# A fused attention and MLP kernel on one core: the second MLP product as seven half-size products, and attention tiles normalised in pairs

## The chip, the core and the metric

The kernel runs on one core of a Trainium2 chip. The core has five engines that work at the same time and meet through semaphores: TensorE (PE, matrix products and transposes, results in PSUM), VectorE (DVE), ScalarE (ACT), GpSimd (POOL) and SyncE (SP, here only a queue that starts DMAs). The metric is the device time of one execution in microseconds. A matmul has a stationary operand, loaded first (row PEld of the profile), and a moving operand that streams past it. PSUM has eight banks of 512 fp32 values per partition.

## The reference

```python
scores = scale * (q @ k.T)                        # batch 8, heads 8, seq 576, head_dim 64
mask_local   = (rel >= 0) & (rel < 32)            # heads 0..3; rel = row - column
mask_strided = (rel >= 0) & (col % 32 == row % 32)  # heads 4..7
attn = softmax(where(mask, scores, -1e9))
x = (attn @ v) -> (4608 tokens, 512)
h = x @ w_in                                      # 512 -> 2048
g = h * tanh(log(1 + exp(h)))                     # "Mish"
out = g @ w_out                                   # 2048 -> 512, float32
```

## The kernel before, in words

The 4608 tokens are worked through in nine blocks of 512 (`for t in range(NBLK)`). Attention is worked through in eight batches of 576 tokens. Batch 0 is a prologue. From then on block t holds the attention of batch t+1 in the gaps of its MLP, so that blocks 0 to 6 carry attention and blocks 7 and 8 carry none. The order on every engine is the order in which the program emits instructions; nothing is reordered by a scheduler.

**A block has two stages.** In the first (`mlp1`, L426) PE makes h in eight groups of two 128-wide slices of the 2048. A group fills one "acc" (two PSUM banks), and ACT turns it into `gT` with one Mish activation (L431). There are three accs, x, y and z, used in turn. In the second stage (`mlp2`, L446) PE makes the output in four tiles of 128 tokens, each of 16 matmuls with 512 moving columns, emitted as 16 steps of four matmuls. After step i the attention pieces of `at[i]` are emitted. Block 8 uses `mlp2_last` (L473).

**Attention pieces.** `Q` (L276) makes scores in an acc, and ACT exponentiates them into P tiles (L281). A part is six or five such units: s0, s1 and s2 of the strided heads, l0, l1 and l2 of the local heads. `M` multiplies a part by the mask (L287, on DVE). `V` (`pv`, L303) multiplies one of 8 strided tiles or 6 local windows by v, four matmuls into one bank of a ring of two (`tile_t`). DVE then takes the reciprocal of the row sums (L314) and scales (L315) into `x_s` or `x_l`. `pv2` does the same for two tiles at once in an acc (L328, L329); before the change only the prologue uses it. `X` (`xt`, L342 and L352) transposes six or eight such tiles on PE into a bank of the ring, and ACT copies them to `xT` (L149), the input of the next `mlp1`.

**Queues.** SP's queue holds in this order for block t: the store of the first two token tiles (L454, after step 7), six DMA transposes of k and q of batch t+2 (L172 and L178, after step 9), the second store, then the loads of k, q and v of batch t+3 (L109, L115, L129). The transposes of the local heads read the bf16 copies that POOL casts (`cast_qk_loc`, `cast_v`, L151) from loaded float32. POOL's queue in block t holds these casts, emitted between the two stages, and then two DMA issues for batch t+3 (`load_qk_str`, L97).

PSUM in the second stage: acc z and one other hold the output, acc x and y take scores.

Of the kernel before, what the change touches and what calls it, by code (L numbers as in the profile page):

```python
# [10 lines left out]
F32 = mybir.dt.float32  # L11
# [27 lines left out]
def kernel(ctx, tc, q, k, v, moe_w_in, moe_w_out, out):  # L39
# [37 lines left out]
    x_l = const.tile([128, NW, 256], BF16, name="x_l")  # L77
    x_s = const.tile([128, CS, 256], BF16, name="x_s")

    g_pool = ctx.enter_context(tc.tile_pool(name="gp", bufs=2))  # L80
    small = ctx.enter_context(tc.tile_pool(name="small", bufs=4))
    o_pool = ctx.enter_context(tc.tile_pool(name="op", bufs=2))
    PS = bass.MemoryType.PSUM
# [277 lines left out]
    def attn_steps(b, x, y):  # L361

        a = Attn(b)
        Q = lambda i_acc, *parts: (lambda: a.qk(parts, i_acc))
        M = lambda kd, i: (lambda: a.mask(kd, i, nc.vector))
        V = lambda kd, i: (lambda: a.pv(kd, i))
        X = lambda kd, hf: (lambda: a.xt(kd, hf))
        s0, s1, sl2, l0, l1 = ("s", 0), ("s", 1), (("s", 2), ("l", 2)), ("l", 0), ("l", 1)
        if x == y:
            return [  # L370
                [], [Q(x, s0)],
                [M(*s0), Q(x, s1)],
                [V("s", 0)],
                [V("s", 1), M(*s1), Q(x, *sl2)],
                [V("s", 2)],
                [V("s", 3), M("s", 2), M("l", 2), Q(x, l0)],
                [V("s", 4)],
                [V("s", 5), M(*l0), Q(x, l1)],
                [V("s", 6), V("l", 5)],
                [V("s", 7), V("l", 0), M(*l1)],  # L380
                [X("s", 0), V("l", 1)],
                [X("s", 1), V("l", 2)],
                [V("l", 3), V("l", 4)],
                [X("l", 0), X("l", 1)], [],
            ]
        return [
            [],
            [Q(x, s0), Q(y, s1), M(*s0), M(*s1)],
            [],
            [V("s", 0), V("s", 1)],  # L390
            [Q(x, *sl2), Q(y, l0), V("s", 2)],
            [V("s", 3), M("s", 2), M("l", 2)],
            [V("s", 4), M(*l0)],
            [Q(x, l1), V("s", 5)],
            [V("s", 6), V("l", 5)],
            [V("s", 7), M(*l1)],
            [V("l", 0), V("l", 1)],
            [X("s", 0), V("l", 2)],
            [X("s", 1), V("l", 3)],
            [V("l", 4), X("l", 0)],  # L400
            [X("l", 1)], [],
        ]


# [7 lines left out]

    def mlp1(t, accs):
        gT = g_pool.tile([128, 16, 512], BF16, tag="gT", name="gT")

        held = {}

        def group(g, ccs=(2, 3, 0, 1)):
            if g not in held:
                held[g] = acc(accs[g % 3], "psh")  # L420
            ps = held[g]
            for u in range(2):
                fc = 2 * g + u
                for a, n, o in segs(t):
                    for cc in ccs:
                        nc.tensor.matmul(  # L426
                            ps[:, u, o:o + n], lhsT=w_in[:, cc, fc * 128:(fc + 1) * 128],
                            rhs=xT[:, cc, a:a + n], start=(cc == 2), stop=(cc == 1),
                        )
            if ccs[-1] == 1:  # L430
                nc.scalar.activation(gT[:, 2 * g:2 * g + 2, :], ps[:], AF.Mish)  # L431
        if t == 0:
            return gT, [lambda g=g, c=c: group(g, c) for c in ((2, 3), (0, 1)) for g in range(2)] + [
                lambda g=g: group(g) for g in range(2, 8)
            ]
        return gT, [lambda g=g: group(g) for g in range(8)]

    def mlp2(t, gT, accs, fc_major=False):
        po = {}
# [43 lines left out]
    with tc.manual_schedule():  # L483
# [12 lines left out]
        load_v_str(0)  # L496
        load_v_loc(0)
        load_qk_loc(1)
        lq0 = g_pool.tile([128, 16, 512], BF16, tag="gT", name="lq0")
        lq0 = lq0[:].rearrange("p a b -> p (a b)")[0:PL]  # L500
        kl0, ql0 = [lq0[:, 1536 * i:1536 * i + 1536].rearrange("p (h x) -> p h x", h=4) for i in range(2)]
        for p in P_l:
# [55 lines left out]
        nc.sync.dma_start(gate[:], w_in[0:1, 0, 1536:1792])  # L558
        load_v(1)
        accs = (2, 1, 0)  # L560
        gT, g1 = mlp1(0, accs)
        a.xt("s", 0)
        a.xt("s", 1)
        Sc.preload_act_table(AF.Mish)
# [21 lines left out]
            cast_v(2, Po, Po)  # L586

        for t in range(NBLK):
            x, y, z = accs
            if t > 0:  # L590
                gT, g1 = mlp1(t, accs)
            ts, at = [], []
            if t == 0:
                ts, at = t_steps(1), attn_steps(1, y, y)
                at[0] = ts[2:4] + [cast_v1]
                at[9].append(lambda: transpose_by_dma(2))
                out_accs, accs = (z, x), (y, z, x)
            else:
                if t + 1 < B:
                    at = attn_steps(t + 1, x, y)  # L600
                if t + 2 < B:
                    at[9].append(lambda: transpose_by_dma(t + 2))
                out_accs, accs = (z, y), (z, x, y)
            for i, g in enumerate(g1):
                g()
                if t == 0:
                    for n in {7: (4, 5), 8: (6, 7), 9: (0, 1)}.get(i, ()):
                        ts[n]()
            if t > 0 and t + 2 < B:
                cast_qk_loc(t + 2, Po, Po)  # L610
                cast_v(t + 2, Po, Po)
            if 0 < t < B - 3:
                load_qk_str(t + 3)
            if t == NBLK - 1:
                mlp2_last(t, gT, (z, y, x))
                break
            for i, g in enumerate(mlp2(t, gT, out_accs, fc_major=(t == 0))):
                g()
                if i < len(at):
                    for s in at[i]:  # L620
                        s()
            if t + 3 < B:
                load_qk_loc(t + 3)
                load_v(t + 3)
# [30 lines left out]
```

## Time and profile before

| what | us |
|---|---|
| median of three runs | 324.11 |
| all runs | 324.11, 325.24, 319.83 |
| profiled execution: span, first to last instruction | 321.4 |
| PE busy in it | 298.8 |
| DVE, ACT, POOL busy | 103.7, 172.6, 78.0 |
| first stage of blocks 1, 2, 3, 5, 6, 7 | 13.81 to 13.82 each |
| second stage of blocks 1, 2, 3, 6 | 18.66 or 18.67 each |
| second stage of blocks 4 and 5 | 19.11, 19.60 |
| second stage of block 7, which has no attention | 13.81 |

Only the span of the profiled execution is recorded; it has no separate device time. It lies between the lowest and the highest of the three runs. A stage is read in the timeline of PE from the first matmul of its line to the first matmul of the next stage. An engine's busy time is an average over stages, so a gain is read from the stage that it falls in. A matmul's listed duration contains its passage through the array, which overlaps with the next one; the pace is the distance of two starts. A few matmul records are missing.

### The profile page before, as it was taken

The page shows a single profiled execution, that of the slowest core. Times are in us where ns is not written, and L with a number is a line of the kernel's source. Part 1 is how long each engine was busy: PE and PEld are TensorE (multiplying, and loading weights), DVE is VectorE, ACT ScalarE, POOL GpSimd, SP SyncE. Part 2 cuts the span into 40 slices and gives each one's busy share as a digit, 9 for nine tenths or more (in the row PEclk, how much of TensorE's full clock was granted, in tenths as well). Part 3 has the DMA queues.
Part 4 walks back from the last instruction along what each step waited for, and adds up shares of the span by engine and source line. Part 5 has one row for each costly group of instructions (what it writes and reads, how often), then busy time and mean ns, then how long its engine had stood idle before and what let it go on. Part 6 is the DMA issues. An engine that isn't in the chain of part 4 may idle for free.

```text
span 321.4 us, 5833 instructions
## 1 busy us (share of the span) xinstructions
PE 298.8 (93%) x2448; PEld 159.8 (50%) x2488; DVE 103.7 (32%) x289; ACT 172.6 (54%) x195; POOL 78.0 (24%) x93
## 2 busy tenths in 40 slices
PE   0678997999999999999999999999999999999995
PEld 0564454544454445444578555444544554444444
DVE  7672066600470047104710381028201830000000
ACT  2572653385737573767375646564667456315601
POOL 9288008322036015304500450035000000000000
PEclk9999999999999999999999999999999999999999
DMA  6999999999999999999999959995800101011012
GB/s 177 215 228 206 223 194 179 188 180 134 226 185 206 110 231 205 191 197 183 203 167 209 192 121 160 193 191 137 147 37 0 67 13 55 0 65 67 0 55 75
DMA packets 103113, 46.71 MB, mean 145 GB/s; under 512 B 85168, under 2 KB 95728, under 8 KB 103088
## 3 DMA queue, kind: packets, MB, share of 16 engines
q1 hardware_dynamic: 91648, 37.22, 65.2%
q0 software_dynamic: 11152, 8.92, 18.8%
q8 instruction: 19, 0.31, 0.4%
q10 hardware_dynamic: 288, 0.21, 0.2%
q14 instruction: 6, 0.05, 0.0%
HBM read 38.34 MB, written 9.44 MB: 149 GB/s over the span
## 4 chain that ended last, share of the span: by engine, by line
PE 74%; DVE 11%; DMA 7%; SPq 3%; issue 2%; ACT 2%; POOL 0%; POOLq 0%; ACTq 0%
PE psh L426 36%; PE pso L446 24%; PE pso L473 4%; PE po L303 4%; DMA vl<-in_v_dram 4%; DMA w_out<-in_moe_w_out_dram 3%; DVE x_l L315 3%; PE ps L276 2%; DVE x_s L315 2%; PE trx L342 2%; DVE ks L151 1%; DVE rden L314 1%; DMA st<-in_k_dram 1%; DVE Pl L287 1%; PE trx L352 1%
## 5 line engine op out<-in xcount | busy, mean ns | idle before, releaser
L426 PE MATMUL psh<-xT,w_in 128*128 128x512 bf16 (+1 forms) x628 | 127.7, 362 | 0.8 <-issue 0.2
L446 PE MATMUL pso<-w_out,gT 128*128 128x512 bf16 x485 | 121.6, 379 | 3.0 <-DMA w_out<-in_moe_w_out_dram 1.4
L431 ACT ACTIVATE gT<-psh 128x1024 bf16<-128x1024 f32 x72 | 73.6, 1023 | 45.4 <-PE psh L426 44.1
L426 PEld LDWEIGHTS <-w_in 128*128 128x128 bf16 x640 | 63.1, 99 | 63.2 <-issue 3.2
L446 PEld LDWEIGHTS <-gT 128*128 128x128 bf16 x512 | 43.6, 97 | 40.4 <-issue 1.5
L287 DVE TENSOR_TENSOR Ps<-Ps,consts_sb 72x864 bf16<-72x864 bf16 (+1 forms) x24 | 16.2, 678 | 114.6 <-ACT Ps L281 114.5
L149 ACT COPY xT<-trx 128x576 bf16<-128x576 bf16 x32 | 20.1, 639 | 37.5 <-PE trx L352 28.0
L151 POOL CAST kl<-kl 96x768 bf16<-96x768 f32 (+1 forms) x13 | 12.2, 960 | 77.6 <-DMA kl<-in_k_dram 77.6
L453 ACT COPY osb<-pso 128x1024 f32<-128x1024 f32 x16 | 16.2, 1012 | 22.6 <-PE pso L446 13.8
L281 ACT ACTIVATE Ps<-ps 72x864 bf16<-72x864 f32 (+1 forms) x24 | 18.5, 804 | 13.8 <-PE ps L276 13.8
L315 DVE TENSOR_TENSOR x_s<-po,rden 72x256 bf16<-72x256 f32 x56 | 23.5, 420 | 1.9
L314 DVE RECIPROCAL rden<-po 72x4 f32<-72x4 f32 (+1 forms) x100 | 17.4, 174 | 18.9 <-PE po L303 18.8
L281 ACT ACTIVATE Pl<-ps 128x960 bf16<-128x960 f32 (+1 forms) x24 | 18.7, 806 | 5.6 <-PE ps L276 5.5
L303 PEld LDWEIGHTS <-Ps 72*128 72x128 bf16 x256 | 14.0, 101 | 13.4 <-DVE Ps L287 3.4
L303 PE MATMUL po<-vs,Ps 72*128 72x65 bf16 x256 | 17.7, 201 | 1.7 <-DVE Ps L287 0.8
L315 DVE TENSOR_TENSOR x_l<-po,rden 96x256 bf16<-96x256 f32 x44 | 18.5, 420 | 1.5
L151 DVE COPY osb<-pso 128x512 f32<-128x512 f32 (+1 forms) x2 | 1.1, 558 | 54.5 <-PE pso L473 54.5
L151 POOL CAST vl<-vl 128x768 bf16<-128x768 f32 x15 | 13.0, 894 | 12.9 <-DMA vl<-in_v_dram 11.3
L303 PE MATMUL po<-vl,Pl 128*128 128x65 bf16 x192 | 12.9, 201 | 2.2 <-POOL vl L151 0.7
L151 POOL CAST vs<-vs 72x2048 bf16<-72x2048 f32 x6 | 11.4, 1893 | 14.5 <-DMA vs<-in_v_dram 10.7
L151 POOL CAST ql<-ql 96x768 bf16<-96x768 f32 (+1 forms) x13 | 11.0, 873 | 15.1 <-DMA ql<-in_q_dram 15.1
L473 PE MATMUL pso<-w_out,gT 128*128 128x512 bf16 (+1 forms) x79 | 14.0, 336 | 0.1
(66 smaller groups left out, 178.3 us busy)
## 6 DMA issues: line engine op xcount, KB each, us to landing
out_dram<-osb SPq DMA_DIRECT2D x16, 512.0 KB, 3.0
vl<-in_v_dram SPq DMA_DIRECT2D x7, 768.0 KB
vs<-in_v_dram SPq DMA_DIRECT2D x8, 576.0 KB
kl<-in_k_dram SPq DMA_DIRECT2D x7, 576.0 KB, 7.6
ql<-in_q_dram SPq DMA_DIRECT2D x7, 576.0 KB, 10.1
w_out<-in_moe_w_out_dram POOLq DMA_DIRECT2D x4, 512.0 KB, 15.7
ks<-in_k_dram POOLq DMA_DIRECT2D x7, 288.0 KB, 8.9
qs<-in_q_dram POOLq DMA_DIRECT2D x7, 288.0 KB, 9.5
```

The costliest lines, as they stand in the source:

```text
L149: nc.scalar.copy(out_, in_)
L151: eng.tensor_copy(out_, in_)
L281: nc.scalar.activation(pt[0:n, :, 0:nw], ps[0:n, :, o0:o0 + nw], AF.Exp, scale=scale)
L287: meng.tensor_tensor(out=pm, in0=pm, in1=mk[0:n, :].unsqueeze(1).unsqueeze(1).to_broadcast([n, 2, nu, w]), op=ALU.mult,)
L303: nc.tensor.matmul(po[:, h, :], lhsT=pt[0:n, c0:c0 + 128], rhs=rhs, start=True, stop=True,)
L314: nc.vector.reciprocal(rden[0:m, :], po[0:m, :, D])
L315: nc.vector.tensor_tensor(out=dst.rearrange("p (h d) -> p h d", h=4), in0=po[0:m, :, 0:D], in1=rden[0:m, :].unsqueeze(2).to_broadcast([m, ...
L426: nc.tensor.matmul(ps[:, u, o:o + n], lhsT=w_in[:, cc, fc * 128:(fc + 1) * 128], rhs=xT[:, cc, a:a + n], start=(cc == 2), stop=(cc == 1),)
L431: nc.scalar.activation(gT[:, 2 * g:2 * g + 2, :], ps[:], AF.Mish)
L446: nc.tensor.matmul(p[:, ot % 2, :], lhsT=gT[:, fc, 128 * ot:128 * ot + 128], rhs=w_out[:, fc, :], start=(fc == 0), stop=(fc == 15),)
L453: nc.scalar.copy(osb[:], p[:])
L473: nc.tensor.matmul(p, lhsT=gT[:, fc, 128 * ot:128 * ot + 128], rhs=w_out[:, fc, c0:c1], start=(fc == 0), stop=(fc == 15),)
```

## The change

- **Seven products.** In blocks 1 to 7 the second product is split in two along tokens, along the 2048 and along the 512 outputs. Instead of eight quarter products (each 8 x 2 matmuls of 256 columns' worth) there are seven, in Strassen's form as Winograd arranges it. Each product is 16 matmuls of 256 moving columns. They run through two halves of acc z, one bank each: `za` takes products 1, 3, 5 and 7, `zc` takes 2, 4 and 6. Products are added up in the bank where the form allows it (a product goes on from what is left there); in between, DVE or ACT copies or adds the bank into the output tile `osb`.
- **Sums.** The form needs four sums of quarters of `gT` (tile `Sg`) in every block, made by DVE in three portions after Mish groups 3, 6 and 7 (`SUMS_AT`), and four sums of quarters of `w_out` (tile `Tw`), made by DVE once, in block 1. So that a portion has its quarters, Mish group g now holds slices g and g+8.
- **Attention in these blocks.** The stage has 14 steps of eight 256-column matmuls. `V` of one tile becomes `V2` of two tiles, all in acc y. The masks of the local parts move from DVE to POOL (`G`). The casts of batch t+2 move from between the stages to after step 9, the transposes by DMA from after step 9 of 16 to after step 10 of 14, and both stores go to the end of the stage (after products 6 and 7).
- **Buffers.** `gT` has one buffer in place of two; `Sg` takes the place of the other.

Block 0, block 8 and the prologue keep their order.

```diff
         return [
-            [],
-            [Q(x, s0), Q(y, s1), M(*s0), M(*s1)],
-            [],
-            [V("s", 0), V("s", 1)],
-            [Q(x, *sl2), Q(y, l0), V("s", 2)],
-            [V("s", 3), M("s", 2), M("l", 2)],
-            [V("s", 4), M(*l0)],
-            [Q(x, l1), V("s", 5)],
-            [V("s", 6), V("l", 5)],
-            [V("s", 7), M(*l1)],
-            [V("l", 0), V("l", 1)],
-            [X("s", 0), V("l", 2)],
-            [X("s", 1), V("l", 3)],
-            [V("l", 4), X("l", 0)],
-            [X("l", 1)], [],
+            [Q(x, s0)],
+            [Q(y, s1), M(*s0)],
+            [M(*s1)],
+            [],
+            [V2("s", 0), Q(x, *sl2)],
+            [M("s", 2), G(*l2)],
+            [V2("s", 2), Q(x, l0)],
+            [G(*l0)],
+            [V2("s", 4), Q(x, l1)],
+            [V2("s", 6), G(*l1)],
+            [V2("l", 0), X("s", 0)],
+            [X("s", 1)],
+            [V2("l", 2), X("l", 0)],
+            [V2("l", 4), X("l", 1)],
         ]
...
+    SUMS_AT = {3: (0, 4), 6: (4, 7), 7: (7, 8)}
+
+    def sums_g(gT, Sg, c0, c1):
+        lo1, lo2 = gT[:, c0:c1, 0:256], gT[:, c0:c1, 256:512]
+        hi1, hi2 = gT[:, 8 + c0:8 + c1, 0:256], gT[:, 8 + c0:8 + c1, 256:512]
+        s1, s2, s3, s4 = [Sg[:, i, c0:c1, :] for i in range(4)]
+        sums(s1, lo2, hi2, ALU.add)
+        sums(s2, s1, lo1, ALU.subtract)
+        sums(s4, hi1, s2, ALU.subtract)
+        sums(s3, lo1, lo2, ALU.subtract)
...
+        def product(ps, lhs, rhs, first, last, after, late=False):
+            def mm(pair, cs):
+                for c in cs:
+                    nc.tensor.matmul(
+                        ps[:, pair, :], lhsT=lhs(c, 128 * pair), rhs=rhs(c),
+                        start=(first and pair == 0 and c == 0), stop=(last and c == 7),
+                        skip_group_check=True,
+                    )
+            if late:
+                return [lambda: mm(0, range(7)), lambda: (mm(1, range(7)), mm(0, (7,)), mm(1, (7,)), after())]
+            return [lambda: mm(0, range(8)), lambda: (mm(1, range(8)), after())]
...
+        steps += product(za, g(0, 0), w(0, 0), True, False, cp(nc.vector, c11, za), late=True)
+        steps += product(zc, sg(0), tw(0), True, False, cp(nc.scalar, c22, zc))
+        steps += product(za, sg(1), tw(1), False, False, cp(nc.scalar, c12, za))
+        steps += product(zc, sg(3), w(1, 1), False, True, lambda: add(c12, zc))
+        steps += product(za, sg(2), tw(2), False, False, lambda: add(c22, za))
+        steps += product(zc, g(1, 0), w(1, 0), True, True, lambda: (add(c11, zc), store(0)))
+        steps += product(za, g(1, 1), tw(3), False, True, lambda: (cast(nc.scalar, c21, za), store(1)))
...
-            if t > 0 and t + 2 < B:
-                cast_qk_loc(t + 2, Po, Po)
-                cast_v(t + 2, Po, Po)
             if 0 < t < B - 3:
                 load_qk_str(t + 3)
...
+                if t > 0 and i == 9 and t + 2 < B:
+                    cast_qk_loc(t + 2, Po, Po)
+                    cast_v(t + 2, Po, Po)
```

`sums` is one DVE `tensor_tensor`; `add` is one that adds a bank to `osb` in place; `cp` is a copy on the engine named. `sums_w` makes `Tw` in four such operations of 2048 elements.

## The prediction

> **What bounds the kernel now.** I read the page's busy shares and chain first, then a table of engine busy time by stage, then the timelines of single engines.
>
> ```profile
> PE 298.8 (93%) x2448; PEld 159.8 (50%) x2488; DVE 103.7 (32%) x289; ACT 172.6 (54%) x195; POOL 78.0 (24%) x93
> ...
> PEclk9999999999999999999999999999999999999999
> ...
> PE 74%; DVE 11%; DMA 7%; SPq 3%; issue 2%; ACT 2%; POOL 0%; POOLq 0%; ACTq 0%
> ```
>
> PE bounds the kernel, at full granted clock. By stage (start:end, length, then busy time and count of PE, PEld, DVE, ACT, POOL, then clock, DMA share, GB/s):
>
> ```profile
> 131.36:145.18 13.82, 13.77 (x65) 6.27 (x64) 0.00 (x0) 9.46 (x9) 1.41 (x3) 1.00 1.21 174
> 145.18:163.85 18.67, 18.24 (x202) 9.85 (x205) 11.04 (x34) 10.29 (x13) 8.72 (x10) 1.00 1.26 192
> 163.85:177.88 14.03, 14.03 (x129) 12.47 (x129) 0.00 (x0) 9.48 (x10) 1.17 (x2) 1.00 1.32 188
> ```
>
> The first stage is 64 matmuls of 512 columns, 13.82 us: 216 ns each. Block 4's is cut into 128 matmuls of 256 columns, because its tokens cross the end of `xT`, and takes 14.03 us: 109.6 ns each, so that halving the columns halves the time although every matmul has its own weight load. A second stage with attention is 18.67 us: 64 x 0.216 = 13.82 of products and 4.85 of attention. In block 2's timeline of PE the starts give for the latter 0.50 for the first 24 score matmuls, 0.54 and 0.32 for the others, 0.13 per `V`, 0.26 per `X`, 0.10 idle ahead of each of three groups of scores, and one wait of 0.28 at 126.3 for a bank of the ring: 4.57 without that wait.
>
> **What the products save.** Removed per block: 64 x 0.216 = 13.82. Added: 7 x 16 x 0.1096 = 12.27. That is 1.55 us per block, 10.9 over seven blocks, all on PE.
>
> The Trainium skill, page "TensorE: Matmul & The Clock Gate", section "Back-to-back issue gap", gives a sustained spacing of about 131 ns for pairs of weight load and matmul at 512 columns and 81 ns at 128. A straight line between them puts 256 columns at some 98 ns (an estimate); by it the stage would go from 8.4 to 11.0 us and the change would lose 2.6 us a block. Block 4 decides otherwise.
>
> **What DVE gets, and whether it is late.** Masks of two operands on 128x960 take 0.64 and on 128x384 0.34: 0.14 plus 0.53 ns per element. So the sums cost 0.68 (1024 elements), 0.55 (768) and 0.28 (256) each, four of each: 6.0 us per block. An operand in PSUM doubles the price per element (72x512 in 0.69); if the sums ran like that they would take 1.21, 0.95 and 0.41. I take 0.53, since `gT` is bf16 in SBUF like the masks. Time 0 is now the start of the second stage. In block 2 Mish 7 ran from 0.20 to 1.22 and Mish 6 ended at -0.50, so sums 4 to 6 run until 1.7 and the last four until 2.85. The copy of product 1 (row of 128x512, 0.69) ends at 3.55, mask s0 at 4.2 (after its exponential, 3.4 as before), s1 at 4.9. PE reaches the last chunk of product 2 at 3.2 (its sum is there at 2.0), product 3 at 4.2 and the first `V2` at 5.1. All of this is hidden, by 0.6 us at its tightest. In block 7, without attention, product 3 comes at 3.5 and waits 0.25. `sums_w` (4 x 1.22) runs in block 1's first stage, where DVE is idle. ACT copies 3 x 0.59 in place of 2 x 1.01. All of the other adds (0.69, like the copy) meet PE two steps later.
>
> **What the pairs cost.** The prologue has `pv2`. In the chain, PE, then the scaling:
>
> ```profile
> 22.36 0.45 PE po L303 x8
> 23.08 0.69 DVE x_l L329
> ```
>
> From the first of eight matmuls (22.36) to the scaled pair (23.77) are 1.41 us, of which PE itself works 0.25; with `V` it was 0.96 for four (128.83 to 129.79). What PE does in the rest decides. The changed order of PE's instructions, with its waits, shows three places:
> - Step 12: `V2("l",2)` and at once `X("l",0)`, whose third transpose needs window 2 of that very pair. PE works 0.25 + 0.08, waits 1.09. Before, windows 0 to 2 lay a step or more ahead.
> - Step 13: the same with window 4 after one transpose: 1.12. Here before `X("l",1)` had a step of four matmuls ahead of it.
> - Step 10: `V2("l",0)` needs acc y back from `V2("s",6)`. On DVE that pair stands behind the add of product 5. Counted from the end of step 9's matmuls: add 0.20 to 0.81, reciprocal, scaling until 1.73. PE is there after 0.26 + 0.88 = 1.14 and waits 0.65.
>
> These are 2.86 us where 0.28 was. Scores in five groups instead of three add 0.20 of switching (between 0 and 0.3). The new stage: 12.27 + 4.57 + 0.20 + 2.86 = 19.90, against 18.67: 1.23 more. In blocks 1 and 2 the next first stage also needs `X("l",1)`'s copy (0.64 on ACT) for its third matmul; the last four products covered it, now two matmuls (0.43) do: 0.45 each, 0.9.
>
> **What the move to POOL costs and cures.** Blocks 4 and 5 were 0.44 and 0.93 longer. The page puts block 5's wait down to POOL's cast of v, but the timelines of DVE and of POOL (start, length, in brackets the idle time before) show a mask held until that cast was over; the second line is the same mask undisturbed in block 6:
>
> ```profile
> 218.44 1.43 DVE L287 TENSOR_TENSOR Ps<-Ps,consts_sb 72x576 bf16<-72x576 bf16 x1
> ...
> 251.79 0.44 DVE L287 TENSOR_TENSOR Ps<-Ps,consts_sb 72x576 bf16<-72x576 bf16 x1
> ```
>
> ```profile
> 217.68 1.89 POOL L151 CAST vs<-vs 72x2048 bf16<-72x2048 f32 x1 [3.38 <-DMA vs<-in_v_dram]
> ```
>
> The casts now start behind `G("l",1)`, when DVE's masks are over and its operations read PSUM, so I count those 1.37 as gone. `G` itself is in no row. Below, 0.64 as on DVE; above, a 960-element mask is ten runs of 96, and if each cost as much as POOL's dearest four-element copy (0.49) above the cast's 1 ns per element, 5.9. I take 2.0, two casts' worth, as the nearest row is the cast (128x768 in 0.80) and a mask reads two operands. Then l0, exponentiated at 9.3, is masked at 11.4, and PE asks at 12.5; l1 at 13.8, asked at 15.7. Hidden; it starts to cost at some 3.1 us each.
>
> The Trainium skill, page "GPSIMD Engine Reference", speaks against this move twice. Its section "Elementwise — side-by-side cycle accounting" has a two-input operation at 2.6 cycles per element, by which a 960-element mask is 2.1 us (an estimate from 1.2 GHz). Its section "Instruction dispatch" has the first call of freshly loaded code pay about 6 us; POOL's order shows one extra instruction ahead of the first `G`, and by that page block 1 would wait 1.9 us more, once. No run here shows either.
>
> **Queues.** Behind the `G`s on POOL stand the casts, from 13.9 to 20.6 (1.6, 1.6, 1.9, 1.6 from their rows), and the two issues for batch t+3, which have a block to spare. On SP the strided transposes go earlier than before, the local ones wait for the casts (from 14.7), and behind these stand both stores and the loads. Block 2's ten issues took 21.2 us and the last load landed 10 later: the loads end near 46 at the latest, while the casts that read them begin at 47.6 and come to v at 51. With the transposes landing ahead of the next scores by more than 10 us, the cover is some 5 us; what goes beyond it lands on PE one for one.
>
> **Sum.** 6 x 1.23 + 0.9 - 1.37, and block 7: 12.27 + 0.25 - 13.82 = -1.30. Together +5.6 on a span of 321.4: 327.0, 1.7% more. On the median of 324.11 this is **329.7**. The span lies inside the runs' 319.83 to 325.24; about 2% is what a measurement here can tell from no change.
>
> **Rivals.**
> - *The waits are hidden and the saving stays.* Stage 12.27 + 4.57 + 0.2 = 17.0: six times -1.6, -1.4, -1.3: 309 of span, 311.5. For it: PE's bound and block 4's pace. Against it: the named operand of the very next instruction, and PE keeps order. 0.08.
> - *The sums run at one element per 1.04 ns* (slower than before). Then the last sum of product 2 is at 3.7, product 1's copy ends at 5.6: PE waits 0.5 and 0.9, 1.4 per block, seven times: +9.8 on top, 339.6. It decides from about 0.7 ns per element. For it: `Sg` and `gT` are read in runs of 256 with gaps. Against it: the masks' rows. 0.10.
> - *`G` is late.* At 5.9 us each PE waits 2.1 and 3.4 more per block, six times: 363; at 4 us the second is 1.7 late in all, 340. 0.05.
> - *The transfers fall behind.* For it: the DMA share is over 1 in blocks 1 to 3, where a round of transposes takes 28.4 us (98.7 to 127.1), and the wait for the casts now breaks it. Against it: a block lasts 33.7. If the round grew to 36, the cover would go in two blocks and four would pay 2.3 each: 339. 0.05.
> - *The products are no cheaper*, the change not doing what it says: 1.55 back, seven times: 341. Block 4 has fresh weights in every matmul too. 0.02.
>
> **Numbers.** The forecast has 0.70. Its own size moves with the waits (2.2 to 3.2 per block instead of 2.86) and the switching (0 to 0.3): 324 to 334, of it 0.47 within 2% and 0.23 beyond. Faster by over 2%: 0.08; within: 0.47; slower: 0.45. The range runs from 322.5, where waits and switching are least and the runs scatter low, to 340, with the half-speed sums in and only the first and the dearest `G` out.
>
> **What will show it.** Right: in blocks 1 to 6 PE idle some 1.1 us twice ahead of L344's transposes with DVE's x_l as releaser, about 0.65 ahead of the first local `V2`; products at 0.11 us; block 7 near 12.5. Wrong: sums over 1 us for 1024 elements, PE waiting for POOL at `Pl`, scores waiting for kTl, or DVE scaling pairs in well under 0.9 us.

## The result, and the profile after

The changed kernel takes **372.77 us** (median; runs 365.74, 371.00, 374.54, 374.61) against 324.68 us for the kernel before in the same runs. The ratio is **1.142, 95% interval 1.125 to 1.159**: slower, by far more than the 1.7% of the forecast and well above the top of its range. The profiled execution of after is one of the two longest, 374.54 us with a span of 372.8, while the ratio is made from the other two; what follows compares stages, and a shorter profile (370.7 of span, of the kernel below that sends block 0's stores through ACT's queue) has the same second stages in blocks 2 to 7, 24.38 to 24.40 and 18.54.

The page of the profile after, its rows of busy time, of granted clock and of the chain of work:

```profile
PE 301.9 (81%) x2824; PEld 197.7 (53%) x2824; DVE 155.4 (42%) x315; ACT 171.1 (46%) x202; POOL 107.2 (29%) x111
...
PEclk9999999996799999999989999999999999999999
...
PE 63%; DVE 17%; ACT 7%; DMA 5%; SPq 4%; issue 3%; ACTq 0%; POOL 0%; DVEq 0%
```

PE has hardly more work than before (301.9 us against 298.8) in a span that is 51.4 us longer: nearly all of the loss is idle time of PE. It was 93% busy and is 81% busy. DVE and ACT, 13% of the chain before, are now 24% of it, and the clock row falls in the tenth and eleventh slices (84 to 102 us) and once more near 190.

The view of what PE waited for in the profile after (line of PE, releaser, us in total, times, longest):

```profile
PE pso L497 <- DVE osb L153: 15.5, 7, 9.8
PE pso L497 <- DVE osb L476: 13.9, 21, 0.9
PE trx L344 <- DVE x_l L331: 11.4, 12, 1.0
PE pso L497 <- ACT osb L151: 9.7, 14, 0.7
```

Three of the four rows are the seven products waiting for a copy or an add of the output: 39.1 us. The third row is the pairs of local windows, which the forecast had counted.

By stage, from the first matmul of one to the first matmul of the next, in us:

| second stage of block | before | after | predicted |
|---|---|---|---|
| 1 | 18.67 | 37.97 | 19.90 |
| 2, 3, 6 | 18.67 | 24.41 to 24.55 | 19.90 |
| 4, 5 | 19.17, 19.59 | 24.39, 24.41 | 19.90 |
| 7, no attention | 13.81 | 18.53 | 12.5 |

Two things have to be explained: some 4.5 us in every block above what was predicted (6.0 in block 7), and 13.6 us more in block 1 alone than in the blocks behind it. The rest of the 51.4 is small: the first stages of blocks 2 and 3 are 0.46 longer each, that of block 4 1.5, and what lies ahead of block 1 is 2.5 shorter.

**The loss of every block** is plainest in block 7, where nothing but products runs. PE's timeline after (start, length, engine, line, operation, in brackets the idle time before and its releaser):

```profile
323.19 1.91 PE L497 MATMUL pso<-w_out,gT 128*128 128x256 bf16 x16
326.64 1.91 PE L497 MATMUL pso<-Tw,Sg 128*128 128x256 bf16 x16 [1.54 <-DVE osb L153]
329.27 1.91 PE L497 MATMUL pso<-Tw,Sg 128*128 128x256 bf16 x16 [0.72 <-ACT osb L151]
331.85 1.91 PE L497 MATMUL pso<-w_out,Sg 128*128 128x256 bf16 x16 [0.67 <-ACT osb L151]
334.60 1.91 PE L497 MATMUL pso<-Tw,Sg 128*128 128x256 bf16 x16 [0.85 <-DVE osb L476]
337.29 1.91 PE L497 MATMUL pso<-w_out,gT 128*128 128x256 bf16 x16 [0.78 <-DVE osb L476]
339.98 1.91 PE L497 MATMUL pso<-Tw,gT 128*128 128x256 bf16 x16 [0.78 <-DVE osb L476]
```

These are the seven products. Each runs at the predicted pace, and ahead of every one but the first PE stands until a copy or an add is over. The one waited for is always that of the product just before. Product 2 writes the other bank than product 1, and yet it begins only when product 1's bank has been copied out (1.54 us, with the sums ahead of that copy on DVE). Product 3 is held by ACT's copy of product 2, not by DVE's copy of product 1. In blocks with attention the same six gaps are 0.83, 0.72, 0.67, 0.85, 0.54 and 0.52: 4.1 us a block, some of them shorter since attention pieces stand between.

**The loss of block 1** is one wait and what it brings. PE's timeline after, block 1:

```profile
77.59 0.93 PE L497 MATMUL pso<-w_out,gT 128*128 128x256 bf16 x7
81.36 0.37 PE L278 MATMUL ps<-qTs,kTs 64*128 64x72 bf16 x12 [2.85 <-DMA qTs<-qs]
...
92.95 3.57 PE L497 MATMUL pso<-Tw,Sg 128*128 128x256 bf16 x16 [9.82 <-DVE osb L153]
```

Product 2 starts 9.82 us late, and its 16 matmuls then take 3.57 us in place of 1.91. What DVE's copy of product 1 itself waited for stands in the chain of work after (start, length, what):

```profile
81.45 1.22 SPq L180
...
82.77 9.34 DMA out_dram<-osb
...
92.20 0.70 DVE osb L153
...
92.95 3.58 PE pso L497 x16
```

The copy writes into an output buffer that the store of block 0 is still reading. There are two such buffers. In the kernel before the first copy of block 1 into one of them ran at 89.14, 9.1 us into the stage; in the seven-product form the first product is copied out after a seventh of the work, and PE was done with it 5.2 us into the stage, the wait for `qTs` included. The store was issued at 82.77, behind the last transpose on SP's queue. Taken together: 9.0 us more idle time ahead of product 2 than in a later block, 2.85 for the scores' operand `qTs`, and 1.7 for matmuls at half clock are the 13.6.

### The profile page after: what moved, and what is told of

It reads as the page before. It is cut to its first block, busy times and chain, and to the rows that moved or that the text cites. A ratio compares the mean times of both kernels' runs of the same rounds, so it can differ in the third digit from the quotient of the medians.

```text
span 372.8 us, 6636 instructions
## 1 busy us (share of the span) xinstructions
PE 301.9 (81%) x2824; PEld 197.7 (53%) x2824; DVE 155.4 (42%) x315; ACT 171.1 (46%) x202; POOL 107.2 (29%) x111
## 4 chain that ended last, share of the span: by engine, by line
PE 63%; DVE 17%; ACT 7%; DMA 5%; SPq 4%; issue 3%; ACTq 0%; POOL 0%; DVEq 0%
PE psh L431 29%; PE pso L497 20%; DVE Sg L449 5%; DVE osb L476 4%; PE pso L552 4%; PE po L305 4%; DVE x_l L331 3%; DMA out_dram<-osb 3%; ACT osb L151 2%; SPq L180 2%; ACT Pl L283 2%; PE ps L278 2%; PE pso L525 2%; DMA w_out<-in_moe_w_out_dram 2%; PE trx L344 2%
## 5 line engine op out<-in xcount | busy, mean ns | idle before, releaser
L289 POOL TENSOR_TENSOR Pl<-Pl,consts_sb 128x960 bf16<-128x960 bf16 (+1 forms) x18 | 29.4, 1636 | 152.7 <-ACT Pl L283 152.7
L497 PE MATMUL pso<-Tw,Sg 128*128 128x256 bf16 x336 | 43.8, 279 | 26.5 <-DVE osb L153 15.5
L497 PEld LDWEIGHTS <-Sg 128*128 128x128 bf16 x448 | 42.9, 99 | 42.0 <-issue 35.0
L449 DVE TENSOR_TENSOR Sg<-gT 128x1024 bf16<-128x1024 bf16 (+2 forms) x48 | 24.3, 520 | 85.9 <-ACT gT L437 85.9
L497 PE MATMUL pso<-w_out,gT 128*128 128x256 bf16 x224 | 28.8, 273 | 4.0 <-DVE osb L476 4.0
L476 DVE TENSOR_TENSOR osb<-pso,osb 128x512 f32<-128x512 f32 x21 | 14.5, 692 | 17.5 <-PE pso L497 14.8
L331 DVE TENSOR_TENSOR x_s<-po,rden 72x512 bf16<-72x512 f32 x28 | 19.2, 686 | 1.0
L497 PE MATMUL pso<-w_out,Sg 128*128 128x256 bf16 x112 | 14.4, 273 | 4.7 <-ACT osb L151 4.7
L497 PE MATMUL pso<-Tw,gT 128*128 128x256 bf16 x112 | 14.3, 272 | 3.9 <-DVE osb L476 3.9
L525 PE MATMUL pso<-w_out,gT 128*128 128x512 bf16 x64 | 16.4, 379 | 0.1
## 6 DMA issues: line engine op xcount, KB each, us to landing
kl<-in_k_dram SPq DMA_DIRECT2D x7, 576.0 KB, 12.5
w_out<-in_moe_w_out_dram POOLq DMA_DIRECT2D x4, 512.0 KB, 13.8
```

The costliest lines, as they stand in the source:

```text
L289: meng.tensor_tensor(out=pm, in0=pm, in1=mk[0:n, :].unsqueeze(1).unsqueeze(1).to_broadcast([n, 2, nu, w]), op=ALU.mult,)
L331: nc.vector.tensor_tensor(out=dst.rearrange("p e (h d) -> p e h d", h=4), in0=po[0:m, :, :, 0:D], in1=rden[0:m].unsqueeze(3).to_broadcast( ...
L449: nc.vector.tensor_tensor(out=out_, in0=in0, in1=in1, op=op)
L476: add = lambda o, p: nc.vector.tensor_tensor(out=o, in0=p, in1=o, op=ALU.add)
L497: nc.tensor.matmul(ps[:, pair, :], lhsT=lhs(c, 128 * pair), rhs=rhs(c), start=(first and pair == 0 and c == 0), stop=(last and c == 7), sk ...
L525: nc.tensor.matmul(p[:, ot % 2, :], lhsT=gT[:, fc, 128 * ot:128 * ot + 128], rhs=w_out[:, fc, :], start=(fc == 0), stop=(fc == 15),)
```

## Experiments

The theory formed from these views: the two banks are two halves of **one tile**, and the program's generated waits order accesses by tile. A product is then made to wait for whatever touched the tile last, though that was the other bank. The list of PE's instructions that carry a wait shows the same without a run (line, operation, tile, engine waited for; products 2 to 7 of one block of the changed kernel):

```
L497 Matmult pso<-Tw,Sg 128x256 [waits DVE]
L497 Matmult pso<-Tw,Sg 128x256 [waits Activation]
L497 Matmult pso<-w_out,Sg 128x256 [waits Activation]
L497 Matmult pso<-Tw,Sg 128x256 [waits DVE]
L497 Matmult pso<-w_out,gT 128x256 [waits DVE]
L497 Matmult pso<-Tw,gT 128x256 [waits DVE]
```

Product 3 (second line) waits for ACT, which does product 2's copy. If waits went by bank it would wait for DVE. The rivals were that the chip itself cannot use one bank while an engine reads the other, and that the pairs of attention tiles make most of the loss.

The main runs in one table. The last column is the part of the profiled span that begins with block 1; what lies ahead of it is the same work in all of them and took between 63.4 and 71.0 us.

| kernel | median us | before beside it | profile from block 1 on |
|---|---|---|---|
| before | 324.68 | | 255.2 |
| after | 372.77 | 324.68 | 309.0 |
| two one-bank tiles | 340.36 | 324.72 | 270.5 |
| two tiles, pieces in another order | 327.48 | 323.52 | 261.2 |
| + pieces a step earlier | 323.65 | 323.52 | 256.7 |
| + three output buffers | 320.33 | 321.95 | 251.8 |
| + ordinary product in block 1 (two buffers) | 319.27 | 323.7 | 250.6 |
| ordinary product in blocks 1 to 7 | 328.66 | 323.52 | 256.1 |

### Two one-bank tiles in place of one of two banks

```diff
-        return ps_a.tile([128, 2, 512], F32, tag=f"acc{i}", name=name)
+        if i == 2 and ps_z:      # acc z, from block 1 on
+            return [ps_z[0].tile([128, 512], F32, tag=f"z{u}", name=name + str(u)) for u in range(2)]
...
-                za, zc = [ps[:, i, :].rearrange("p (n o) -> p n o", n=2) for i in range(2)]
+                za, zc = [part(ps, i)[:, 0:512].rearrange("p (n o) -> p n o", n=2) for i in range(2)]
```

`part` picks a tile; nothing of the arithmetic or the order changes. A Mish on acc z becomes two of 512. The two tiles also lie in another pair of PSUM banks, 6 and 7 in place of 4 and 5, which was not tested apart.

> The changed kernel with one edit: from block 1 on, acc z is two tiles of one bank each in place of one tile of two banks (its Mish becomes two activations of 512). The banks, the matmuls and the copies stay as they are. Theory A (the program waits: both halves lie in one tile, so each product waits for the copy or add of the product before it, although that one reads the other bank): the idle of 0.5 to 0.85 us ahead of each product goes, stages with attention fall from 24.5 to about 20, block 7's from 18.5 to 12.5, and the whole from 372.8 of span to about 340; the 9.8 us in block 1, where the copy of product 1 waits for a store, stay for the most part. Rival B (the chip: a bank cannot be written while its neighbour is read, or a product that goes on in a bank has to drain first): the idle stays, 366 to 373. Rival C (the pairs of attention tiles and their order are the main loss): within 5 us of 370.

Measured: 340.36 us, 32.4 less; the profile's span falls from 372.8 to 337.9. PE's timeline of block 7 in this kernel:

```profile
294.64 1.91 PE L509 MATMUL pso<-w_out,gT 128*128 128x256 bf16 x16
296.38 3.66 PE L509 MATMUL pso<-Tw,Sg 128*128 128x256 bf16 x32
299.88 1.91 PE L509 MATMUL pso<-w_out,Sg 128*128 128x256 bf16 x16
301.62 1.91 PE L509 MATMUL pso<-Tw,Sg 128*128 128x256 bf16 x16
303.37 1.91 PE L509 MATMUL pso<-w_out,gT 128*128 128x256 bf16 x16
305.12 1.91 PE L509 MATMUL pso<-Tw,gT 128*128 128x256 bf16 x16
```

The seven products (the second row holds two) follow each other at 1.74 us without a gap, and the stage is 12.22 us: the 12.27 of the forecast. The same copies and adds still run, from one bank while PE writes the other. So the chip did not ask for the waits; the tile did. The list of instructions with waits now has product 3 waiting for DVE and product 4 for ACT, each two products back, and products 6 and 7 with no wait of their own.

The Trainium skill, page "PSUM — Partial Sum Buffer", section "PSUM bank collisions raise a hardware error", asks that engines be kept apart by bank (or by bank and quarter of the partitions). This pair of kernels agrees: waits by bank were enough, and waits across two banks cost 4.3 us a stage (24.41 to 20.11).

What is left is, per attention block, the pairs, as PE's timeline of block 2 of the same kernel shows:

```profile
137.80 0.42 PE L313 MATMUL po<-vl,Pl 128*128 128x65 bf16 x8 [0.58 <-DVE x_s L339]
...
141.77 0.34 PE L352 MATMUL trx<-consts_sb,x_l 96*128 96x96 bf16 x4 [0.93 <-DVE x_l L339]
...
144.26 0.39 PE L352 MATMUL trx<-consts_sb,x_l 96*128 96x96 bf16 x5 [0.97 <-DVE x_l L339]
```

These are the three places of the forecast, priced there at 0.65, 1.09 and 1.12.

### Where block 1 loses its time: the store

Three runs go after the output buffer. In the first and second, block 0's stores go out from ACT's queue and not behind the transposes on SP's; the first is on the changed kernel, the second on the one with two tiles.

```diff
-                nc.sync.dma_start(out[r:r + 256, :].rearrange("(o p) d -> p o d", o=2), osb[:])
+                (nc.scalar if t == 0 else nc.sync).dma_start(
+                    out[r:r + 256, :].rearrange("(o p) d -> p o d", o=2), osb[:]
+                )
```

> The changed kernel with one edit: the two stores of block 0 are issued from ACT's queue, where they do not stand behind the six DMA transposes on SP's queue. Theory (the copy of product 1 in block 1 needs the output buffer that those stores still read): the 9.8 us of PE idle at 83 to 93 us and the low granted clock after it go, 361 of span in place of 372.8, all other stages the same. Rival (the transfers of block 1 are late anyway, because the DMA share is over 1): PE waits at the same place for something else, 370 or more.

> Both edits. If the two causes add up: about 328, which is what the forecast had without them, with 1.1 us of PE idle twice per attention stage ahead of the transposes of local windows, and 0.6 ahead of the first local pair. If the forecast's own sum was wrong as well: outside of 322 to 334.

Measured: 377.38 (ratio 1.157, 1.143 to 1.171) and 346.16 (1.068, 1.057 to 1.078). Both are worse than without the edit, by 4.6 and 5.8 us, where a gain was expected. The wait ahead of product 2 did go, to 0.84 in the first of them and to nothing in the second. But the timeline of ACT in the second shows what took its place:

```profile
72.71 0.43 ACTq L545 DMA_DIRECT2D out_dram<-osb  x1
73.17 1.18 ACT L159 COPY xT<-trx 128x576 bf16<-128x576 bf16 x2 [10.05 <-DMA vl<-in_v_dram]
...
85.82 0.42 ACTq L545 DMA_DIRECT2D out_dram<-osb  x1
86.27 1.28 ACT L449 ACT_TABLE_LOAD   x1 [11.00 <-DMA qTs<-qs]
```

ACT did nothing else for 10.05 and 11.00 us up to each of the two issues. These are waits of the program: in the list of ACT's instructions a wait for a DMA semaphore stands ahead of either store, and what had last counted that semaphore up is the load of `vl` for the first store and the transpose into `qTs` for the second, the two transfers in the brackets. ACT's copies and Mish activations stood behind; PE waited 9.21 and 7.16 us for `xT` and `gT`. As a test of the output buffer these two runs are inconclusive, since the wait was moved rather than taken away.

The third run leaves block 0's stores out of the changed kernel.

```diff
-                nc.sync.dma_start(out[r:r + 256, :].rearrange("(o p) d -> p o d", o=2), osb[:])
+                if t > 0:
+                    nc.sync.dma_start(out[r:r + 256, :].rearrange("(o p) d -> p o d", o=2), osb[:])
```

> The changed kernel without the two stores of block 0: rows 0 to 511 of the output are not written, nothing else is left out. Moving those stores to ACT's queue in e2_store0 put ACT itself to waiting. Theory (product 1's copy in block 1 waits for the buffer that the stores read): the 9.8 us before product 2 in block 1 go, and the half granted clock behind it, 361 to 363 against 372.8. Rival (block 1's transfers are late anyway and PE waits for them at the next place): 368 or more.

Measured: 364.9 us where 361 to 363 were expected, ratio 1.132 (1.125 to 1.139). PE's timeline of block 1:

```profile
81.82 0.55 PE L278 MATMUL ps<-qTs,kTs 64*128 64x72 bf16 x12 [2.73 <-DMA qTs<-qs]
...
85.18 1.91 PE L497 MATMUL pso<-Tw,Sg 128*128 128x256 bf16 x16 [0.31 <-DVE osb L153]
```

The 9.82 are 0.31, product 2 runs in 1.91 again, and the stage goes from 37.97 to 28.19. The wait for `qTs` stays (2.73), and here the nine matmuls behind it are slow (2.10 us; 1.16 in the kernel after). That the store is the cause of the long wait is shown, and the slow matmuls of product 2 go with it; the two together are 9.8 of block 1's 13.6. How long the wait is in other executions of the changed kernel is not known: the medians differ by 7.9 us, and the ratios, 1.142 and 1.132, by some 3.5 us only.

### The order of the attention pieces

If the pairs are late because the next instruction needs them at once, a step of products between `V2` and `X` should cure it. The first of three orders, on the kernel with two tiles:

```diff
             [V2("l", 0), X("s", 0)],
-            [X("s", 1)],
-            [V2("l", 2), X("l", 0)],
-            [V2("l", 4), X("l", 1)],
+            [V2("l", 2), X("s", 1)],
+            [V2("l", 4), X("l", 0)],
+            [X("l", 1)],
```

It ran with the store of block 0 on ACT's queue, and without it:

> Both edits, and the last pieces of attention in another order: pair l2 in step 11, pair l4 in step 12 with the transposes of windows 0 to 2, those of windows 3 to 5 in step 13, so that each pair has a step of eight matmuls before its transposes. If the pairs' scaling behind the last matmuls costs what the forecast had (1.09 and 1.12 per block): 1.6 to 2.0 us per block less, six times, 317 to 319, below the kernel before. If DVE is then late elsewhere: 324 to 328.

> The kernel of e1_split with the last attention pieces in another order: pair l2 in step 11, pair l4 in step 12 with the transposes of windows 0 to 2, those of windows 3 to 5 in step 13. Theory (a pair takes 1.4 us from its first matmul to its scaled tiles, and PE waits for what a step of eight matmuls does not cover): the two idle times of 0.93 and 0.97 in e1's timeline go, about 0.2 remains at the second pair, stages of 20.1 come down to 18.4, the whole from 340.4 to 330. If DVE is late anyway: 336 or more.

Measured: 332.9 and 327.48 us, 13.3 and 12.9 less than the same kernels in the old order; the 317 to 319 expected of the first were missed, and it still has ACT's waits for block 0's stores. Not all of the 12.9 is the order's: from block 1 on the profile is 9.3 shorter (270.5 to 261.2), 8.4 of it in the second stages of blocks 2 to 6, and 3.1 lie ahead of block 1, in work that is the same. The second stage of blocks 2 to 6 goes from 20.11 to between 18.27 and 18.49; the two waits of 0.93 and 0.97 are gone but for 0.17, that of 0.58 stays. The ratio to the kernel before is 1.014 (1.009 to 1.020) for the second.

The next order takes care of the third wait too, by having the strided pairs one step earlier:

```diff
-            [G(*l0)],
-            [V2("s", 4), Q(x, l1)],
-            [V2("s", 6), G(*l1)],
+            [V2("s", 4), G(*l0)],
+            [Q(x, l1), V2("s", 6)],
+            [G(*l1)],
             [V2("l", 0), X("s", 0)],
-            [V2("l", 2), X("s", 1)],
+            [X("s", 1), V2("l", 2)],
```

> As e5_x_later, and pairs s4 and s6 a step earlier too (s4 in step 7, s6 behind the scores of step 8), so that the first local pair no longer waits for the scaling of s6 behind the add of product 5 (0.58 in e1). Theory: stages near 17.8, that is below the 18.67 of the kernel before, the whole near 326. If the wait only moves to pair s6, which then stands behind the add of product 4: as e5.

Measured: 323.65 us, ratio 1.004 (0.999 to 1.009). The stage is 17.84 to 18.07, for the first time shorter than the 18.66 before; two waits of 0.25 and 0.22 are left in it. In block 1 5.77 us still go on the output buffer, now ahead of product 3, which goes on in the bank that the copy of product 1 has to read first.

### What the seven products are worth

The last kernel with the ordinary second product in blocks 1 to 7 (64 matmuls of 512 columns, spread over the same 14 steps, in the same two banks), without `Sg` and `Tw`:

```diff
-                steps = mlp2_seven(t, gT, Sg, za, zc)
+                steps = mlp2_plain(t, gT, ps)
```

> e6_earlier with the ordinary second product in blocks 1 to 7: 64 matmuls of 512 columns spread over the 14 steps, two tiles of one bank in turn, no sums and no adds; the sums of w_out are left out too. Theory (seven products are worth the difference of paces, 13.82 against 12.27 us per block, once nothing waits between them): 8 to 11 us above e6. Rival (what the sums, copies and adds cost on DVE and ACT eats the saving even without the serial waits): within 3 us of e6 or below it.

Measured: 328.66 us, ratio 1.018 (1.013 to 1.024), 5.0 more than with seven products, where 8 to 11 were expected. The median misleads here. From block 1 on the two profiles, one of each kernel, are nearly equal, 256.1 and 256.7 us; the 5.0 lie ahead of block 1, in work that both kernels share (71.0 against 64.8 us, with waits for a mask and for the load of `w_out` whose cause was not followed). By stage the seven products are worth 1.59 in block 7 (12.23 against 13.82) and 0.75 to 0.98 in the blocks with attention (17.84 to 18.07 against 18.81 to 19.04), where the waits of 0.25 and 0.22 take most of the missing half. That is 6.3 in all, with 0.5 of shorter first stages, and block 1 takes it back: 26.27 in place of 18.82. The 256.1 against 255.2 of the kernel before say besides that pairs, masks on POOL and the new order of pieces together are worth next to nothing.

### Block 1 set right, in two ways

The ordinary product in block 1 alone, seven in blocks 2 to 7:

```diff
-                steps = mlp2_seven(t, gT, Sg, za, zc)
+                steps = mlp2_plain(t, gT, ps) if t == 1 else mlp2_seven(t, gT, Sg, za, zc)
```

> e6_earlier with the ordinary second product in block 1 (spread over the 14 steps as in e7_plain) and seven products in blocks 2 to 7. In e6 the second stage of block 1 lasts 26.3 us because product 1's copy waits for a buffer of block 0's store; in e7 it lasts 18.8, since the first copy comes four steps later, and the stages of blocks 2 to 7 in e6 are 17.8 to 18.1 against 18.67 before and 12.2 against 13.8. Theory (block 1's wait is the last of what keeps e6 level with the kernel before): 7.5 us below e6, 314 of span, 316 in time, ratio about 0.975. If the wait comes back in block 2: 320 or more.

Measured: 319.27 us over six runs (315.9 to 323.51), ratio **0.989 (0.982 to 0.997)**. The profile's span is 314.0, as expected; the median is some 3 us above, and the expected ratio of 0.975 lies outside the interval. From block 1 on the profile is 5.4 us shorter than with the ordinary product throughout: the seven products bring 6.5 in blocks 2 to 7, and block 1 takes 1.1 longer (19.92 against 18.82).

A third output buffer in place of that:

```diff
-    o_pool = ctx.enter_context(tc.tile_pool(name="op", bufs=2))
+    o_pool = ctx.enter_context(tc.tile_pool(name="op", bufs=3))
```

> The kernel with two one-bank tiles and the attention pieces moved earlier (span 321.5, second stage of block 1 26.27 us, of it 5.77 in one wait ahead of product 2 for the store of block 0), with three output buffers in place of two and nothing else changed. Theory A (block 1 loses its time to the output buffer, whose first use in the seven-product form comes before the store of block 0 has read it): the wait of 5.77 goes to below 0.5. The stage does not get to the 18.06 of the later blocks, since other waits of block 1 stay (some 2.5 us, mask and transposes), so about 20.5; span near 316, median near 318, ratio 0.98 to 0.99. Rival (the store only marks a queue of transfers that is behind; what waits next is the strided transposes): the wait moves to the scores' operands, block 1 stays over 24 us, span 319 or more, ratio 1.00.

Measured: 320.33 us over twelve runs (316.29 to 322.12), ratio **0.993 (0.989 to 0.997)**, span 315.9. The row of the wait with two buffers, from PE's timeline of block 1 in the kernel before this edit, is product 3 and not, as the expectation has it, product 2:

```profile
88.87 1.86 PE L509 MATMUL pso<-Tw,Sg 128*128 128x256 bf16 x8 [5.77 <-DVE osb L161]
```

With three buffers these 5.77 are gone and the stage of block 1 falls from 26.27 to 21.11, so the buffer was what held it; the ratio is just short of the expected 0.98 to 0.99. PE's timeline of block 1 shows what is left:

```profile
80.31 0.37 PE L286 MATMUL ps<-qTs,kTs 64*128 64x72 bf16 x12 [1.52 <-DMA qTs<-qs]
...
87.86 1.03 PE L509 MATMUL pso<-w_out,Sg 128*128 128x256 bf16 x8 [1.52 <-ACT osb L159]
```

The second row is product 4. It waits for ACT's copy of product 2, and that copy goes into block 1's second buffer, which with three in turn is the one that the first store of block 0 still reads. The clock row is at 9 throughout. For both versions the interval ends just below 1, a gain that is smaller than the 2% or so that a measurement here can tell. They were not run together, so nothing here says which is better.

### The local masks back on DVE

```diff
-        G = lambda kd, i: (lambda: a.mask(kd, i, nc.gpsimd))
+        G = lambda kd, i: (lambda: a.mask(kd, i, nc.vector))
```

> e6_earlier with the masks of the local parts on DVE as in the kernel before, in the same steps. DVE gets 1.63 us more per block, two of its 0.65 ahead of a pair's scaling, and POOL's casts, no longer behind the masks, can start while DVE masks and sums. If the forecast was right that POOL's masks (2.0 us in the trace) are hidden and spare DVE: stages 0.5 to 1.5 us longer, 327 to 333 in all. If the masks' engine does not matter: within 2 us of 323.7.

Measured, on the kernel with the earlier order (323.65): four runs of 322.05 to 330.37 us, median 328.81, too far apart for a ratio; the lowest is no longer than the four with the masks on POOL (322.66 to 324.94). The profile is of the run of 329.87. In it blocks 2 to 5 take 18.34, 19.16, 20.16 and 19.53, up to 2.1 more than with the masks on POOL, and block 6 takes 18.07, the same. Block 6 has the same masks and no casts. DVE's and then POOL's timeline of block 4 in this kernel:

```profile
189.47 1.86 DVE L461 TENSOR_TENSOR Sg<-Sg,gT 128x256 bf16<-128x256 bf16 x1
191.37 0.29 DVE L461 TENSOR_TENSOR Sg<-gT,Sg 128x256 bf16<-128x256 bf16 x1
...
191.78 0.68 DVE L161 COPY osb<-pso 128x512 f32<-128x512 f32 x1
```

```profile
189.25 1.95 POOL L161 CAST vs<-vs 72x2048 bf16<-72x2048 f32 x1
```

With no `G` ahead of them on POOL's queue the casts run while DVE makes its sums. A sum of 256 elements takes 1.86 in place of 0.29, until the cast beside it is over, and product 3 waits 1.78 for the copy behind. So in this execution the masks' own time on DVE was free, as block 6 shows, and what their place on POOL is good for is to delay the casts. The median is in the expected range, but for this other reason. Whether every execution loses it is not shown, and the run of 322.05 speaks against it.

## Why the prediction was wrong, point by point

**The step that failed is "What DVE gets, and whether it is late".** It has product 3 wait for product 1's copy alone, "All of the other adds (0.69, like the copy) meet PE two steps later", and "All of this is hidden, by 0.6 us at its tightest". That took the two banks for two buffers. They are one tile, and every product met the copy or add of the product just before it, with little or nothing of PE's work between. The split takes 4.3 off each stage of blocks 2 to 6 (24.41 to 20.11), 6.3 off block 7 (18.53 to 12.22) and 10.1 off block 1 (37.97 to 27.86), where 2.3 of it are a shorter wait for `qTs`. From block 1 on the profile is 38.5 us shorter; the median fell by 32.4, and in the profile what lies ahead of block 1 was 3.7 longer. It could be read beforehand: the order of PE's instructions has product 3 wait for ACT, where two steps' distance asks for DVE. None of the rivals was this; the nearest (sums at half speed) had the place, the first products held by DVE's copy, and another reason.

**A second step was missing.** The change copies product 1 into the output buffer when a seventh of the products is done; "Queues" counts the stores as something behind which loads stand and not as readers of a buffer. In block 1 that cost 9.8 us in the profiles of the changed kernel with and without block 0's stores (37.97 and 28.19), and 5.2 in the kernel with the earlier order, where a third buffer took them away (26.27 and 21.11). In the later blocks no copy waits for a store: a whole first stage (13.8 us) lies between the last product and the next copy.

**"Queues": the cover.** The strided transposes were said to land more than 10 us ahead of the scores. In block 1 they did not: scores come after the first step, and PE waited 2.85 us there, though only there.

**What held.**
- *Products at 0.1096 us.* Measured in block 7 of the split kernel: 16 in 1.74, 0.109 each, for both operands' strides. The stage took 12.22 where 12.27 plus a wait of 0.25 was predicted, and that wait is not there. The estimate of 98 ns from the skill's page was too low here, as block 4 had said.
- *Sums.* Predicted 0.68, 0.55 and 0.28 us; measured 0.69, 0.56 and 0.29 in the timeline of DVE. The rival with half speed was wrong.
- *Pairs.* 1.09, 1.12 and 0.65 predicted, 0.93, 0.97 and 0.58 measured, and each at its place. With them the stage of the split kernel is 20.11, against 19.90: 12.22 of products and 2.48 of these waits leave 5.41 for the attention pieces, 0.6 more than the 4.77 that the forecast had. That the total came so close is in part luck, since waits that were 0.4 shorter made up for more than half of it. The order with a step between cured them, as their cause demands.
- *`xT`.* The first stages of blocks 2 and 3 are 14.27, 0.46 longer; 0.45 was predicted.
- *POOL.* The masks, in the timeline of POOL after:

```profile
99.99 0.91 POOL L289 TENSOR_TENSOR Pl<-Pl,consts_sb 128x384 bf16<-128x384 bf16 x1 [17.44 <-ACT Pl L283]
103.18 2.00 POOL L289 TENSOR_TENSOR Pl<-Pl,consts_sb 128x960 bf16<-128x960 bf16 x1 [2.28 <-ACT Pl L283]
```

  2.00 us where 2.0 was taken, and hidden: PE never waits for `Pl` in blocks 1 to 6. The page "GPSIMD Engine Reference" of the Trainium skill, section "Elementwise — side-by-side cycle accounting", had led to 2.1 and agrees. The 6 us that its section "Instruction dispatch" gives a first call cost nothing here: the first row above is the kernel's first mask on POOL, and it takes 0.91 and starts 0.08 after the exponential that it waits for. Whether they were spent unseen in the 17.44 us that POOL was idle before, no row shows.
- *Contention.* The 1.37 that casts cost masks in blocks 4 and 5 (1.42 by the table of stages above, which has 19.17 where the table ahead of the prediction has 19.11) are gone as counted: after the change those stages are as short as the others (24.39 and 24.41). In the profile with the masks back on DVE the casts cost 5.2 over blocks 2 to 5, there through the sums too.

Put together: from block 1 on the forecast was 255.2 + 5.6 = 260.8, and without the tile's waits the profile shows 270.5. Of the 9.7 between them 8.0 are block 1 (27.86 in place of 19.90), 1.0 the five other stages (20.11 in place of 19.90) and 1.0 the first stage of block 2 (15.25 in that run, its first 3 us at half clock), less 0.3 in block 7.

## What to carry to other kernels

The waits that are generated for such a program go by tile: a buffer that is meant to work as two must be two tiles, and whether it does is read from the engine named in the wait of each chain's first instruction, before any run. When results are written out earlier than before, find the transfer that last read that output buffer and when it lands. And two tiles computed at once need other work between them and their first reader; put that step in with the pairing; it was worth some 9 us here.

## What the runs showed of the hardware

**The clock fell behind long waits, and a few times behind short ones.** The windows of the profile after (start:end, length, busy time and count of PE, PEld, DVE, ACT, POOL, then granted clock, DMA share, GB/s), first around the wait of 9.82 us, then at the beginning of block 4's first stage:

```profile
92.90:97.00 4.10, 3.57 (x16) 2.31 (x16) 1.02 (x2) 0.40 (x1) 0.00 (x0) 0.50 1.13 175
97.00:115.80 18.80, 14.07 (x198) 11.71 (x198) 8.66 (x18) 6.23 (x11) 12.10 (x12) 1.00 0.96 150
```

```profile
193.00:195.00 2.00, 2.00 (x14) 1.44 (x12) 0.00 (x0) 0.64 (x1) 1.15 (x2) 0.50 0.85 315
195.00:197.00 2.00, 2.00 (x15) 1.60 (x14) 0.00 (x0) 0.44 (x1) 0.00 (x0) 0.71 0.96 201
```

The first row is half clock right behind an idle stretch of nearly 10 us, the second full clock again. The Trainium skill, page "TensorE: Matmul & The Clock Gate", section "What's actually happening", has the clock halved after an idle window of about 3.4 us and full again after as long a busy one; the first pair of rows agrees with it. The second pair has no long wait before it, only gaps of up to 1 us, of which the last two are the waits of 0.93 and 0.97 for local pairs, and it cost block 4 about 1.5 us. Two other profiles have the same right behind these two waits: the two-tile kernel in the first stage of block 2 (15.25 in place of 14.27) and the kernel without block 0's stores in that of block 5 (14.94; granted clock 0.50 from 222 to 225 us). No profile of a kernel with a step between the pairs and their transposes has it. Why these stages and not the others is open.

**POOL's casts stop some of DVE's operations and not others.** The sum that reads two operands from SBUF grew from 0.29 to 1.86 us beside a cast. Not every such operation does: in the kernel before, a mask of 384 elements took its 0.34 at 120.67 and one of 960 its 0.65 at 220.61, both beside casts from end to end. Operations that read PSUM kept their time: in the kernel after, five adds into `osb` and 15 scalings of local pairs ran for more than half of their time beside casts, all in 0.69 as without. The skill's page "GPSIMD Engine Reference", section "Specifications", has POOL contend for SBUF with VectorE operations of two SBUF inputs, which fits the sum and the operations that were spared for reading PSUM.
